# VectorE alone makes z and the late weights' low parts, in a new order of its queue

## The chip, the core and the metric

The kernel runs on one core of a Trainium2 chip. Its five queues (TensorE, VectorE, ScalarE, GpSimd, and SyncE for the transfers) each run their own instructions strictly in order and wait for one another through semaphores. The metric is the device time of one execution in microseconds; the text calls a time a median where it is one of several runs. In the profile PE is TensorE, PEld its weight loads, DVE VectorE, ACT ScalarE, POOL GpSimd, SP SyncE.

## The reference

Three layers, one after the other, on 4 sequences of 768 tokens and 384 channels:

```python
for t in range(S):                      # attention, 8 heads of 48
    y[:, :, t] = einsum(q[:, :, t], state)
    v_old = einsum(state, kt)
    state = state + bt * outer(kt, vt - v_old)
...
theta = x @ w_theta                     # mixing
zr, zi = x * np.cos(theta), x * np.sin(theta)
y = einsum('ts,bsd->btd', w_tok_r, zr) + einsum('ts,bsd->btd', w_tok_i, zi)
u = x + y
x = u + np.maximum(u @ w_ch, 0.0)
...
xn = (x - mu) / np.sqrt(var + 1e-06) * g_ln   # feed-forward
out = x + np.maximum(xn @ w_ch1, 0.0) @ w_ch2
```

The weights come as float64, the rest as float32.

## The kernel before

**Precision.** Each large product runs as three products of reduced-precision operands: a value is split into a high part (`hi`, `zh`, `xh`, a converting copy on ScalarE) and a low part (`lo`, `zl`, `xl`, the value minus its high part), and high x high, high x low and low x high are summed.

**Weights** (class `Weights`). The float64 words are turned to float32 on the chip, in units of two tiles of 128 x 384 (768 wide). A unit goes through three stages: its raw words are loaded and ScalarE takes their magnitude (`magnitude`, L759; in the attention VectorE does it itself, L755); VectorE clamps and merges the bits (`low`: two clamps, L765 and L766, two merges, L775 and L776); `parts` makes the high part (ScalarE, L789) and the low part (L794, VectorE or GpSimd by `split`). A call of `pump` moves each unit by one stage; a call of `step`, used in the attention, does half as much. `finish` does the last stage alone. Units of the mixing weights are called w0 to w5 by the tile of 128 source tokens that they serve, two units each. A unit of the feed-forward weights is only merged, multiplied by g on GpSimd (L784) and stored to memory (`stash`), to be loaded again as f0, f1, ... later.

**Attention.** Chunks c = 0 to 23 of 32 tokens. In each, `R` subtracts what the state already holds (VectorE's `Rs`, L427), for two halves of the heads, and the state's update on TensorE and ScalarE hangs on it. Between the halves a function `late(c, k)`, k = 0, 1, 2, puts preparations for the mixing into the queues.

**Mixing** (class `Mixer`, loop over 24 steps in `build`). The list MIX orders the steps: for each of four sequences b the source tiles s = 0, 1, 2, then for each the tiles 3, 4, 5. Step i multiplies z of (b, s) into six sums y, in two halves of 18 matmuls. Around that, the loop prepares ahead: `trans` transposes x of step i + 3, `theta` multiplies x of step i + 2 with w_theta, `angles` takes the fraction of a turn (`kk`, `nf`), `sines` and `cosines` evaluate it on ScalarE, and `turn` makes z of step i + 1 from it. After each third step the sums y go into u on VectorE and ScalarE (L929, L927). In the last steps the loop also starts the first column block of the feed-forward part (`pre`: parts, three products with the channel weights, mean, centring, square, reciprocal of the deviation).

**Feed-forward.** For eight column blocks and twelve weight tiles an up product, its positive part (`hh`, `hl`), and a down product.

The order of the loop's calls is the order of each queue. The numbers of calls in a step stand in two lists: PA[i] pumps before the first half of step i, PB[i] after its preparations.

Of the kernel before, what the change touches and what calls it, by code (L numbers as in the profile page):

```python
# [660 lines left out]
MAGIC = 12582912.0  # L661
# [11 lines left out]
class Weights:  # L673
# [32 lines left out]
    def pump(self):  # L706

        self.finish()
        for u in self.one:
            self.low(*u)  # L710
        self.one, self.two = [], self.one
        self.load()
        if self.loaded:
            u = self.loaded.pop(0)
            self.one.append(self.magnitude(*u))
        self.load()
        for dst, t in self.stores:
# [60 lines left out]
    def parts(self, u, raw, t, clamped):  # L778
        nc = self.nc
        self.ready.add(u[0])  # L780
        if len(u) == 5:
            dst, g = u[3:]
            w = t[:, 0].rearrange("p (k c) -> p k c", k=KB)
            nc.gpsimd.tensor_tensor(out=w, in0=w, in1=bc(g.unsqueeze(2), [128, KB, 128]), op=ALU.mult)  # L784
            self.stores.append((dst, t))
            return
        hi, lo, scale, split = u[3:]
        if scale is None:
            nc.scalar.copy(out=hi, in_=t)  # L789
            n = t.shape[1]  # L790
            split = n if split is None else split
            for e, r in ((nc.gpsimd, slice(0, split)), (nc.vector, slice(split, n))):
                if r.stop > r.start:
                    e.tensor_tensor(out=lo[:, r], in0=t[:, r], in1=hi[:, r].bitcast(F32), op=ALU.subtract)  # L794
        else:
            nc.scalar.activation(out=hi, in_=t, func=AF.Copy, scale=scale)
            nc.vector.scalar_tensor_tensor(out=lo, in0=t, scalar=scale, in1=hi.bitcast(F32), op0=ALU.mult, op1=ALU.subtract)


class Mixer:  # L800
# [19 lines left out]
    def load_w(self, s, wtok, pool, wts, w=None):  # L820
        w = self.W[s] = w or [pool.tile([128, 4, C], F32R, name=f"w{s}_{i}") for i in range(2)]
        for q in range(2):
            wts.add(("w", s, q), wtok[s, q], w[0][:, 2 * q:2 * q + 2], w[1][:, 2 * q:2 * q + 2], split=0 if s < 3 else None)
# [42 lines left out]
    def angles(self, i):  # L866
# [4 lines left out]
        nc.vector.tensor_scalar(out=kk, in0=ps, scalar1=MAGIC, scalar2=None, op0=ALU.add)  # L871
# [17 lines left out]
    def turn(self, i):  # L889
# [6 lines left out]
        nc.gpsimd.tensor_tensor(out=zf[:, 1], in0=zf[:, 1], in1=xs, op=ALU.mult)  # L896
        nc.vector.tensor_tensor(out=zf[:, 0], in0=zf[:, 0], in1=xs, op=ALU.mult)  # L897
        for q in range(2):
            nc.scalar.copy(out=zh[:, q], in_=zf[:, q])  # L899
            nc.gpsimd.tensor_tensor(out=zl[:, q], in0=zf[:, q], in1=zh[:, q].bitcast(F32), op=ALU.subtract)  # L900
        self.Z[i] = zh, zl

# [171 lines left out]
class Spare:  # L1074


    def __init__(self, st):
        self.st, self.n = st, 0

    def tile(self, shape, dt, name):  # L1080
        if name == "tot":
            return self.st.tile([128, 2, C], dt, name="t", bufs=3)[:, 0]
        if self.n % (4 * C) == 0:
            self.n = 0
            self.t = self.st.tile([128, 2 * C, 2], U32, name="raw", bufs=2).rearrange("p c t -> p (c t)")
        self.n += shape[1]
        return self.t[:, self.n - shape[1]:self.n].bitcast(dt)


def build(tc, a):  # L1090
# [8 lines left out]
    with tc.manual_schedule(), outer:  # L1099
# [14 lines left out]
        def late(c, k):  # L1114
# [16 lines left out]
            if (c > 19 or (c, k) == (19, 1)) and k < 2:  # L1131
# [51 lines left out]
        SLOTS = {"uh": 2, "ul": 3, "xh": 0, "xl": 1}  # L1183
# [17 lines left out]
        for i in range(n):  # L1201
# [32 lines left out]
            if i == 21:  # L1234
                two_f(0, *[slot(f"f0_{k}", 6 + k, [128, 4, C], F32R) for k in range(2)])
# [3 lines left out]
            for k in {15: (0,), 19: (4,), 20: (5,), 21: (6,), 22: (7,)}.get(i, ()):  # L1239
# [65 lines left out]
```

## Time and profile before

| what | value |
|---|---|
| median of three runs | 804.92 us (803.36 to 805.32) |
| the profiled execution | 804.83 us, of which the profile's span is 802.6 us |
| TensorE busy | 718.3 us, 89% of the span; granted clock 0.964 on average |
| VectorE busy | 527.6 us, 66% |
| ScalarE busy | 347.2 us, 43% |
| GpSimd busy | 302.7 us, 38% |

The span begins at the first instruction; all positions in the text are microseconds from there. Busy time of TensorE includes matmuls at half clock, so a busy TensorE may still lose time. The shares are averages over three layers with different limits, so the text goes by stretches of time.

### The profile page before, as it was taken

How to read it: one execution, taken by the hardware profiler on the slowest of the kernel's cores; microseconds unless marked ns; L12 is line 12 of the kernel's file. 1: busy time of each engine (PE TensorE's matmuls, PEld its weight loads, DVE VectorE, ACT ScalarE, POOL GpSimd, SP SyncE). 2: the span in 40 equal slices, each digit the busy share in tenths (PEclk: the TensorE clock that was granted, in tenths of full speed). 3: DMA queues.
4: the chain of work that ended last, by engine and by line, in shares of the span. 5: the costliest groups of instructions: out<-in, count | busy, mean ns of one | idle time of the engine just before them, and what ended most of it. 6: DMA issues, size and time to landing. Idle time of an engine off the chain costs nothing.

```text
span 802.6 us, 19216 instructions
## 1 busy us (share of the span) xinstructions
PE 718.3 (89%) x8059; PEld 658.3 (82%) x8062; DVE 527.6 (66%) x865; ACT 347.2 (43%) x783; POOL 302.7 (38%) x305
## 2 busy tenths in 40 slices
PE   4687877777777699999899899999999999999997
PEld 2465555554577689999799799999999999999997
DVE  5899899986778988889766645535343443444342
ACT  1276777687855455563434434222322222231310
POOL 4855655642223666565432533312111112112110
PEclk7599999999999999999999999999999999999999
DMA  9776657333453333433410220000000000000000
GB/s 269 222 206 187 208 165 223 90 83 120 152 177 119 119 105 93 127 130 101 155 40 21 98 84 16 31 1 31 1 30 0 31 1 20 11 1 30 1 30 29
DMA packets 29717, 71.41 MB, mean 89 GB/s; under 512 B 4928, under 2 KB 17472, under 8 KB 29632
## 3 DMA queue, kind: packets, MB, share of 16 engines
q1 hardware_dynamic: 29632, 70.19, 28.2%
q8 instruction: 63, 1.03, 0.5%
q14 instruction: 22, 0.18, 0.1%
HBM read 56.02 MB, written 9.44 MB: 82 GB/s over the span
## 4 chain that ended last, share of the span: by engine, by line
PE 53%; DVE 26%; ACT 8%; issue 6%; POOL 5%; DMA 1%; SPq 0%; ACTq 0%; DVEq 0%; POOLq 0%
PE ph L1034 19%; PE acc L1053 19%; PE pc L975 5%; DVE t L775 4%; PE y L920 4%; DVE t L776 3%; DVE prod L356 3%; ACT bdw L439 2%; DVE t L766 2%; DVE XT L365 2%; DVE t L765 2%; PE pth L862 1%; DVE zf L897 1%; POOL prodp L372 1%; POOL prodp L356 1%
## 5 line engine op out<-in xcount | busy, mean ns | idle before, releaser
L920 PE MATMUL y<-w,zh 128*128 128x384 f32 x576 | 157.6, 347 | 10.5 <-ACT w L789 7.1
L1053 PE MATMUL acc<-hh,f 128*128 128x384 f32 x576 | 147.0, 336 | 0.0
L1039 DVE SCALAR_TENSOR_TENSOR hl<-ph,hh 128x384 fp32r<-128x384 f32 x96 | 52.5, 554 | 114.8 <-ACT hh L1038 114.8
L1038 ACT ACTIVATE hh<-ph 128x384 fp32r<-128x384 f32 x96 | 46.8, 491 | 167.8 <-PE ph L1034 167.8
L920 PEld LDWEIGHTS y<-w,zh 128*128 128x128 f32 x576 | 108.0, 194 | 12.6 <-ACT w L789 7.8
L1034 PE MATMUL ph<-xh,f 128*128 128x384 f32 x576 | 116.4, 337 | 1.7 <-DVE u L929 1.7
L1053 PEld LDWEIGHTS acc<-hh,f 128*128 128x128 f32 x576 | 104.5, 188 | 0.0
L1034 PEld LDWEIGHTS ph<-xh,f 128*128 128x128 f32 x576 | 101.9, 188 | 2.0 <-issue 2.0
L920 PE MATMUL y<-w,zl 128*128 128x384 f32 x288 | 101.1, 351 | 1.0 <-POOL zl L900 0.6
L1053 PE MATMUL acc<-hl,f 128*128 128x384 f32 x288 | 96.9, 336 | 0.0
L900 POOL TENSOR_TENSOR zl<-zf,zh 128x384 fp32r<-128x384 f32 x48 | 64.5, 1365 | 50.7 <-ACT zh L899 50.7
L1034 PE MATMUL ph<-xl,f 128*128 128x384 f32 x288 | 65.7, 336 | 0.0
L439 ACT COPY bdw<-RW 32x192 f32<-32x192 f32 x192 | 59.6, 310 | 10.2 <-PE RW L435 7.6
L920 PEld LDWEIGHTS y<-w,zl 128*128 128x128 f32 x288 | 57.2, 199 | 2.6 <-POOL zl L900 2.6
L452 ACT COPY bds<-S 48x384 f32<-48x384 f32 x92 | 43.6, 474 | 29.7 <-PE S L447 28.3
L896 POOL TENSOR_TENSOR zf<-zf,x 128x384 f32<-128x384 f32 x24 | 27.4, 1141 | 73.3 <-ACT zf L879 73.2
L1053 PEld LDWEIGHTS acc<-hl,f 128*128 128x128 f32 x288 | 54.0, 188 | 0.0
L447 PE MATMUL S<-bdw,ktt 128*48 128x192 f32 x368 | 41.4, 348 | 13.8 <-ACT bdw L439 13.8
L1063 POOL TENSOR_TENSOR o<-u,o 128x384 f32<-128x384 f32 x21 | 20.8, 1021 | 85.0 <-DVE o L1062 85.0
L1034 PEld LDWEIGHTS ph<-xl,f 128*128 128x128 f32 x288 | 51.6, 188 | 0.0
L435 PEld LDWEIGHTS RW<-Rs,pt 32*32 32x32 f32 x1472 | 19.4, 107 | 30.8 <-DVE Rs L427 24.2
L447 PEld LDWEIGHTS S<-bdw,ktt 128*48 128x48 f32 x368 | 20.5, 126 | 27.8 <-ACT bdw L439 21.7
(159 smaller groups left out, 1342.4 us busy)
## 6 DMA issues: line engine op xcount, KB each, us to landing
kqt<-kq SPq DMA_DIRECT2D x20, 512.0 KB, 6.7
raw<-wtok SPq DMA_DIRECT2D x12, 768.0 KB, 4.3
raw<-wff SPq DMA_DIRECT2D x12, 768.0 KB, 5.0
bdk<-kq SPq DMA_DIRECT2D x40, 192.0 KB, 4.0
vt<-vin SPq DMA_DIRECT2D x24, 192.0 KB, 4.4
ktt<-ktok SPq DMA_DIRECT2D x24, 192.0 KB, 4.2
x<-ys SPq DMA_DIRECT2D x96, 48.0 KB, 2.8
flat<-t SPq DMA_DIRECT2D x12, 384.0 KB, 5.5
```

The lines of the kernel that those rows point to most:

```text
L356: eng.tensor_tensor(out=pr[:, j], in0=bc(lhs[:, j].unsqueeze(2), [128, i, c, kk]), in1=bc(rhs[:, j].unsqueeze(1), [128, i, c, kk]), op=ALU ...
L439: nc.scalar.copy(out=b[rr, :, r, :], in_=RW[h][rr, 1, :, :])
L447: nc.tensor.matmul(S_ps[h][64 * e:64 * e + D, g, :], KT[c][:, 2 * h + g, e, :], b[:, 2 * g + e, :, :], start=(c == 0 and g == 0), stop=Tru ...
L452: nc.scalar.copy(out=n[ee, :, e, :], in_=S_ps[h][ee, :, :].rearrange("p g (r d) -> p (g r) d", r=4))
L775: v.scalar_tensor_tensor(out=i, in0=raw[:, :, 1], scalar=0xC0000000, in1=i, op0=ALU.bitwise_and, op1=ALU.bitwise_or)
L900: nc.gpsimd.tensor_tensor(out=zl[:, q], in0=zf[:, q], in1=zh[:, q].bitcast(F32), op=ALU.subtract)
L920: nc.tensor.matmul(self.Y[q], l[:, ri, 128 * k:128 * k + 128], self.W[s][w][:, 2 * ri + h], start=(first and w == ri == 0 and l is zh), st ...
L975: nc.tensor.matmul(ps, self.wc[w][:, k, 128 * e:128 * e + 128], r[:, k], start=(n == 0), stop=(n == 8))
L1034: nc.tensor.matmul(ps, w[:, 0, 128 * k:128 * k + 128], r[:, k], start=(n == 0), stop=(n == 8))
L1038: nc.scalar.activation(out=hh, in_=ps, func=AF.Relu)
L1039: nc.vector.scalar_tensor_tensor(out=hl, in0=ps, scalar=0.0, in1=hh.bitcast(F32), op0=ALU.max, op1=ALU.subtract)
L1053: nc.tensor.matmul(self.ACC[j][e], w[:, 1, 128 * e:128 * e + 128], r, start=(f == 0 and n == 0), stop=(f == NF - 1 and n == 2))
```

## The change

`turn` multiplies both halves of z by x in one VectorE instruction and converts them in one ScalarE instruction; the subtraction for zl becomes `rest`, one VectorE instruction that stands behind the pumps of the step. `kk` moves from VectorE to ScalarE. The low parts of w0 and w1 go to GpSimd, those of w2 to w5 to VectorE. `pump` issues the high parts first, then clamps and merges, then the low parts, so that `parts` now returns the low part as a function. `finish` leaves the middle of the step. `step` is called at k = 2 too, the extra pumps of the first four steps (PB) fall away, and step 0 makes three before its first half (PA); the feed-forward tiles f0 and f1 are taken up in step 17 instead of 21, and mean, centring, square and reciprocal each come one step later.

```diff
     def pump(self):
-        self.finish()
+        lows = [self.parts(*u) for u in self.two]
         for u in self.one:
             self.low(*u)
         self.one, self.two = [], self.one
+        for f in lows:
+            f()
         self.load()
...
-                e.tensor_tensor(out=lo[:, r], in0=t[:, r], in1=hi[:, r].bitcast(F32), op=ALU.subtract)
+            def low():
+                for e, r in ((nc.gpsimd, slice(0, split)), (nc.vector, slice(split, n))):
+                    if r.stop > r.start:
+                        e.tensor_tensor(out=lo[:, r], in0=t[:, r], in1=hi[:, r].bitcast(F32), op=ALU.subtract)
...
-            wts.add(("w", s, q), wtok[s, q], w[0][:, 2 * q:2 * q + 2], w[1][:, 2 * q:2 * q + 2], split=0 if s < 3 else None)
+            wts.add(("w", s, q), wtok[s, q], w[0][:, 2 * q:2 * q + 2], w[1][:, 2 * q:2 * q + 2], split=0 if s > 1 else None)
...
-        nc.vector.tensor_scalar(out=kk, in0=ps, scalar1=MAGIC, scalar2=None, op0=ALU.add)
+        nc.scalar.activation(out=kk, in_=ps, func=AF.Identity, bias=self.magic)
...
-        nc.gpsimd.tensor_tensor(out=zf[:, 1], in0=zf[:, 1], in1=xs, op=ALU.mult)
-        nc.vector.tensor_tensor(out=zf[:, 0], in0=zf[:, 0], in1=xs, op=ALU.mult)
-        for q in range(2):
-            nc.scalar.copy(out=zh[:, q], in_=zf[:, q])
-            nc.gpsimd.tensor_tensor(out=zl[:, q], in0=zf[:, q], in1=zh[:, q].bitcast(F32), op=ALU.subtract)
+        nc.vector.tensor_tensor(out=zf, in0=zf, in1=bc(xs.unsqueeze(1), [128, 2, C]), op=ALU.mult)
+        nc.scalar.copy(out=zh, in_=zf)
         self.Z[i] = zh, zl
+        self.ZF2 = zf
+
+    def rest(self, i):
+        zh, zl = self.Z[i]
+        self.nc.vector.tensor_tensor(out=zl, in0=self.ZF2, in1=zh.bitcast(F32), op=ALU.subtract)
...
-            if (c > 19 or (c, k) == (19, 1)) and k < 2:
+            if c > 19 or (c, k) == (19, 1):
                 wts.step()
...
                 mx.turn(0)
+                mx.rest(0)
...
-        SLOTS = {"uh": 2, "ul": 3, "xh": 0, "xl": 1}
+        SLOTS = {"uh": 2, "ul": 3, "xh": 6, "xl": 7}
...
-        PA = [2] + [1] * 21 + [2] * 2
-        PB = [1] * 4 + [0] * 14 + [1] * 4 + [2] * 2
+        PA = [3] + [1] * 21 + [2] * 2
+        PB = [0] * 18 + [1] * 4 + [2] * 2
...
             for _ in range(PA[i]):
                 wts.pump()
+            if i + 1 < n:
+                mx.rest(i + 1)
             mx.mix(i, 0, yp)
-            wts.finish()
...
-            if i == 21:
-                two_f(0, *[slot(f"f0_{k}", 6 + k, [128, 4, C], F32R) for k in range(2)])
+            if i == 17:
+                two_f(0, *[slot(f"f0_{k}", k, [128, 4, C], F32R) for k in range(2)])
...
-            for k in {15: (0,), 19: (4,), 20: (5,), 21: (6,), 22: (7,)}.get(i, ()):
+            if i == 15:
+                wp.pool = ff.sp = Spare(mx.cst, ("w1_0", "w1_1"))
+            for k in {15: (0,), 20: (4,), 21: (5,), 22: (6,), 23: (7,)}.get(i, ()):
                 todo[k]()
```

What is left out moves the small tiles of `pre` into the tiles of w1, which are free by then, and keeps a feed-forward tile from being loaded before it is stored. Lines behind the edit shift by up to 16: the merges are L781 and L782 after, the clamps L771 and L772, Rs stays L427.

What the change moves is seen best on VectorE's queue, at three places. First the attention, from the second half of chunk 20 to the first half of chunk 22. Before:

```order
L427 TENSOR_TENSOR Rs_3763<-vt,RW_127 128x192
L797 SCALAR_TENSOR_TENSOR tw_3568<-t,tw_3567 128x768
L755 TENSOR_SCALAR t<-raw 128x384
L765 TENSOR_SCALAR t<-t 128x384
L766 TENSOR_SCALAR t<-t 128x384
L848 TENSOR_TENSOR xl<-pt,xh 128x384
L427 TENSOR_TENSOR Rs_3836<-vt,RW_126 128x192
L775 SCALAR_TENSOR_TENSOR t<-raw,t 128x384
L776 SCALAR_TENSOR_TENSOR t<-raw,t 128x384
L427 TENSOR_TENSOR Rs_3888<-vt,RW_127 128x192
```

And after:

```order
L807 SCALAR_TENSOR_TENSOR tw_3570<-t,tw_3569 128x768
L761 TENSOR_SCALAR t<-raw 128x384
L771 TENSOR_SCALAR t<-t 128x384
L772 TENSOR_SCALAR t<-t 128x384
L781 SCALAR_TENSOR_TENSOR t<-raw,t 128x384
L782 SCALAR_TENSOR_TENSOR t<-raw,t 128x384
L861 TENSOR_TENSOR xl<-pt,xh 128x384
L427 TENSOR_TENSOR Rs_3840<-vt,RW_126 128x192
L807 SCALAR_TENSOR_TENSOR tw_3570<-t,tw_3569 128x384
L761 TENSOR_SCALAR t<-raw 128x768
L771 TENSOR_SCALAR t<-t 128x768
L772 TENSOR_SCALAR t<-t 128x768
```

The next row there is `Rs_3898`. The merges of the second theta unit moved ahead of an Rs, and the clamps of the first unit of w0 (128x768) now stand ahead of the Rs of chunk 21's second half.

Second, step 0 of the mixing, from z of step 1 on. Before (w_1_3699 is the low part of w1, nf that of step 2):

```order
L897 TENSOR_TENSOR zf<-zf,x_70 128x384
L775 SCALAR_TENSOR_TENSOR t<-raw,t 128x768
L776 SCALAR_TENSOR_TENSOR t<-raw,t 128x768
L794 TENSOR_TENSOR w_1_3699<-t,w_0_3698 128x768
L765 TENSOR_SCALAR t<-t 128x768
L766 TENSOR_SCALAR t<-t 128x768
L775 SCALAR_TENSOR_TENSOR t<-raw,t 128x768
L776 SCALAR_TENSOR_TENSOR t<-raw,t 128x768
L794 TENSOR_TENSOR w_1_3699<-t,w_0_3698 128x768
```

After (w_1_4259 is the low part of w2):

```order
L909 TENSOR_TENSOR zf<-zf,x_70 128x768
L771 TENSOR_SCALAR t<-t 128x768
L772 TENSOR_SCALAR t<-t 128x768
L781 SCALAR_TENSOR_TENSOR t<-raw,t 128x768
L782 SCALAR_TENSOR_TENSOR t<-raw,t 128x768
L771 TENSOR_SCALAR t<-t 128x768
L772 TENSOR_SCALAR t<-t 128x768
L781 SCALAR_TENSOR_TENSOR t<-raw,t 128x768
L782 SCALAR_TENSOR_TENSOR t<-raw,t 128x768
L802 TENSOR_TENSOR w_1_4259<-t,w_0_4258 128x768
L916 TENSOR_TENSOR zl<-zf,zh 128x768
L885 SCALAR_TENSOR_TENSOR nf<-kk,pth 128x384
```

The units of w1 are gone from here, two units of w2 stand in their place, and zl of step 1, which GpSimd made before, stands behind them.

Third, a middle step with a unit of the feed-forward weights. Before:

```order
L897 TENSOR_TENSOR zf<-zf,x_71 128x384
L765 TENSOR_SCALAR t<-t 128x768
L766 TENSOR_SCALAR t<-t 128x768
L775 SCALAR_TENSOR_TENSOR t<-raw,t 128x768
L776 SCALAR_TENSOR_TENSOR t<-raw,t 128x768
L871 TENSOR_SCALAR kk<-pth 128x384
L872 SCALAR_TENSOR_TENSOR nf<-kk,pth 128x384
L852 TENSOR_TENSOR u_65<-u_65,pt 128x3x128
L848 TENSOR_TENSOR xl<-pt,xh 128x384
```

After:

```order
L909 TENSOR_TENSOR zf<-zf,x_71 128x768
L771 TENSOR_SCALAR t<-t 128x768
L772 TENSOR_SCALAR t<-t 128x768
L781 SCALAR_TENSOR_TENSOR t<-raw,t 128x768
L782 SCALAR_TENSOR_TENSOR t<-raw,t 128x768
L916 TENSOR_TENSOR zl<-zf,zh 128x768
L885 SCALAR_TENSOR_TENSOR nf<-kk,pth 128x384
L865 TENSOR_TENSOR u_65<-u_65,pt 128x3x128
L861 TENSOR_TENSOR xl<-pt,xh 128x384
```

z is whole, zl is new in the queue, kk has left it.

## Rows read from the trace of the kernel before

**Rows 1.** Busy time by stretch: us, then each engine's, granted clock, transfers.

```profile
core 0: us, PE busy (x) PEld busy (x) DVE busy (x) ACT busy (x) POOL busy (x), PEclk, DMA share, GB/s
196.00:225.00 29.00, 22.74 (x588) 15.86 (x588) 21.95 (x37) 24.78 (x63) 5.74 (x4) 1.00 0.38 118
225.00:303.00 78.00, 62.61 (x319) 59.61 (x320) 67.43 (x80) 40.11 (x73) 39.13 (x26) 0.91 0.40 139
303.00:382.70 79.70, 79.70 (x469) 79.00 (x468) 70.32 (x97) 41.09 (x81) 48.52 (x40) 1.00 0.37 108
436.00:458.40 22.40, 19.17 (x95) 17.22 (x93) 11.44 (x14) 10.24 (x16) 12.54 (x12) 0.92 0.25 89
458.40:802.60 344.20, 340.02 (x1945) 339.70 (x1945) 151.89 (x266) 88.83 (x174) 65.70 (x63) 1.00 0.06 20
```

**Rows 2.** The chain of waits, 385 to 460 us: start, us, what.

```profile
390.61 7.83 PE y L920 x36
...
400.00 1.56 PE pth L862 x9
401.56 0.33 PE pt L835 x3
401.89 6.26 PE y L920 x36
```

**Rows 3.** TensorE in order of time; in brackets idle time before, and releaser.

```profile
236.87 0.61 PE L920 MATMUL y<-w,zh 128*128 128x384 f32 x1 [3.10 <-ACT w L789]
...
390.06 0.55 PE L835 MATMUL pt<-ident,x 128*128 128x128 f32 x3 [3.02 <-DVE u L977]
...
458.36 0.93 PE L1034 MATMUL ph<-xh,f 128*128 128x384 f32 x4 [1.72 <-DVE u L929]
```

**Rows 4.** Busy time by stretch, just after the second of these waits.

```profile
390.60:394.00 3.40, 3.40 (x13) 3.40 (x12) 2.60 (x6) 2.04 (x4) 1.01 (x1) 0.50 0.90 227
```

**Rows 5.** VectorE in order of time, one steady step.

```profile
303.39 1.67 DVE L775 SCALAR_TENSOR_TENSOR t<-raw,t 128x768 uint32<-128x768 uint32 x1
...
307.25 0.55 DVE L872 SCALAR_TENSOR_TENSOR nf<-kk,pth 128x384 f32<-128x384 f32 x1
...
309.59 0.56 DVE L897 TENSOR_TENSOR zf<-zf,x 128x384 f32<-128x384 f32 x1 [1.32 <-POOL zf L896]
```

**Rows 6.** VectorE in order of time, early in the mixing.

```profile
232.82 0.55 DVE L765 TENSOR_SCALAR t<-t 128x768 f32<-128x768 f32 x1
...
235.00 0.96 DVE L776 SCALAR_TENSOR_TENSOR t<-raw,t 128x768 uint32<-128x768 uint32 x1
236.85 0.96 DVE L794 TENSOR_TENSOR w<-t,w 128x768 fp32r<-128x768 f32 x1 [0.90 <-ACT w L789]
237.73 0.55 DVE L765 TENSOR_SCALAR t<-t 128x768 f32<-128x768 f32 x1
```

**Rows 7.** GpSimd in order of time, in the steady step of rows 5.

```profile
302.92 3.02 POOL L900 TENSOR_TENSOR zl<-zf,zh 128x384 fp32r<-128x384 f32 x2 [1.25 <-ACT zh L899]
```

**Rows 8.** VectorE in order of time, end of the attention.

```profile
202.66 0.35 DVE L427 TENSOR_TENSOR Rs<-vt,RW 128x192 f32<-128x192 f32 x1 [0.72 <-PE RW L424]
...
216.96 0.35 DVE L427 TENSOR_TENSOR Rs<-vt,RW 128x192 f32<-128x192 f32 x1
```

**Rows 9.** SyncE's transfer queue in order of time.

```profile
200.28 0.53 SPq L699 DMA_DIRECT2D raw<-wtok  x1
...
227.47 1.92 SPq L699 DMA_DIRECT2D raw<-wtok  x2
```

**Rows 10.** Transfers by line: count, size, median us from issue to landing.

```profile
raw<-wtok SPq DMA_DIRECT2D x12, 768.0 KB, 4.3
```

**Rows 11.** ScalarE in order of time, end of the attention.

```profile
224.46 0.48 ACT L479 COPY ys<-py 128x384 f32<-128x384 f32 x1 [0.30 <-PE py L473]
```

**Rows 12.** VectorE in order of time, end of the mixing.

```profile
451.01 0.55 DVE L1016 TENSOR_SCALAR raw<-pst 128x384 f32<-128x384 f32 x1
...
456.42 1.33 DVE L1021 SCALAR_TENSOR_TENSOR rs<-t,rs 128x384 f32<-128x384 f32 x1 [1.13 <-POOL t L1020]
```

More of the change, by code (lines that the diff above doesn't have):

```diff
@@ L692, in load @@
         while self.todo and len(self.loaded) < (1 if self.more is None else 2):
+            if self.stores and not self.todo[0][2]:
+                return
             u = self.todo.pop(0)
@@ L718, in pump @@
             self.nc.sync.dma_start(out=dst, in_=t)
-        self.stores = []
+        if self.stores:
+            self.stores = []
+            self.load()
     def finish(self):
         for u in self.two:
-            self.parts(*u)
+            self.parts(*u)()
         self.two = []
@@ L785, in parts @@
             self.stores.append((dst, t))
-            return
+            return lambda: None
         hi, lo, scale, split = u[3:]
@@ L791, in parts, with low @@
             split = n if split is None else split
-            for e, r in ((nc.gpsimd, slice(0, split)), (nc.vector, slice(split, n))):
-                if r.stop > r.start:
-                    e.tensor_tensor(out=lo[:, r], in0=t[:, r], in1=hi[:, r].bitcast(F32), op=ALU.subtract)
+            def low():
+                for e, r in ((nc.gpsimd, slice(0, split)), (nc.vector, slice(split, n))):
+                    if r.stop > r.start:
+                        e.tensor_tensor(out=lo[:, r], in0=t[:, r], in1=hi[:, r].bitcast(F32), op=ALU.subtract)
         else:
             nc.scalar.activation(out=hi, in_=t, func=AF.Copy, scale=scale)
-            nc.vector.scalar_tensor_tensor(out=lo, in0=t, scalar=scale, in1=hi.bitcast(F32), op0=ALU.mult, op1=ALU.subtract)
+            def low():
+                nc.vector.scalar_tensor_tensor(out=lo, in0=t, scalar=scale, in1=hi.bitcast(F32), op0=ALU.mult, op1=ALU.subtract)
+        return low
 class Mixer:
@@ L814, in load_theta @@
         self.nc.gpsimd.memset(self.halfpi, HALF_PI)
+        self.magic = self.cst.tile([128, 1], F32, name="magic")
+        self.nc.gpsimd.memset(self.magic, MAGIC)
         self.tw = [self.cst.tile([128, KB, C], F32R, name=f"tw{i}") for i in range(2)]
@@ L1074, with __init__ @@
 class Spare:
-    def __init__(self, st):
-        self.st, self.n = st, 0
+    def __init__(self, pool, tags):
+        self.t = [pool.tile([128, 4, C], F32R if i == 0 else F32, name=t, tag=t) for i, t in enumerate(tags)]
+        self.n = [0, 0]
     def tile(self, shape, dt, name):
[L1081 to L1087, printed above, removed]
+        k = 0 if dt == F32R else 1
+        n = self.n[k]
+        self.n[k] += 1
+        return self.t[k][:, n]
 def build(tc, a):
@@ L1193, in build @@
         n = len(MIX)
-        PA = [2] + [1] * 21 + [2] * 2
-        PB = [1] * 4 + [0] * 14 + [1] * 4 + [2] * 2
+        PA = [3] + [1] * 21 + [2] * 2
+        PB = [0] * 18 + [1] * 4 + [2] * 2
         wp = Late()
-        wp.pool = ff.sp = Spare(wts.st)
         todo = first_pre = ff.pre(0, big, wp, psa)
```

## The prediction

> **What bounds the kernel now.** I read the busy time by stretch first [rows 1]. It splits the program in four. Until 225 us runs the attention. From 225 to 458 us runs the mixing, from 458 us to the end the feed-forward part, where TensorE is busy 340.0 of 344.2 us; the change moves only what stands at that part's very start, so I count the rest as it is. In the mixing TensorE is busy 79.7 of 79.7 us between 303 and 383 us, but only 62.6 of 78.0 us before, and 19.2 of 22.4 us at the end. Busy there is not full speed either: the granted clock is 0.91 in the early stretch. VectorE is busy 67.4 of the 78.0 us of the early stretch.
>
> How long would TensorE need if it never waited? The chain of waits shows its pieces [rows 2]: 36 mixing matmuls 6.26 us, a theta product of nine 1.56 us, three transposes 0.33 us, so 8.15 us for a full step, at the full clock of 2.4 GHz. 20 full steps of that (steps 1 to 20), step 21 without a transpose (7.8), steps 22 and 23 without theta (12.5), three products with the channel weights of the size of a theta (4.7) and two small sums (0.7) make 188.8 us after step 0, and with step 0 about 197. The stretch took 458.4 - 225.0 = 233.4 us. So 36 us are lost in it, and that is the most that the change can gain there.
>
> Where they go: TensorE waits for weight tiles, 3.10 us in one place, for a transpose buffer that VectorE frees late, 3.02 us, and 1.72 us at the start of the feed-forward part [rows 3]. After the 3.02 us the same 36 matmuls took 7.83 us [rows 2], with a granted clock of 0.50 [rows 4], the level of 1.2 GHz: the wait cost 1.57 us again. Behind all these waits stands VectorE. In a steady step it passes each of the two merges of the float64 words (L775, L776) in some 1.67 us [rows 5], while the same operation takes 0.96 us elsewhere [rows 6]. In the slow case GpSimd is in its subtraction for zl, 302.92 to 305.94 us [rows 7].
>
> **The change on VectorE, step by step.** GpSimd loses both halves of the z subtraction and the half multiplication. So the merges should go at 0.96 us, 1.4 us less for the pair. VectorE takes over z whole and zl whole; a 768-wide two-input operation passes in 0.88 us (236.85 to 237.73) [rows 6], so zl adds 0.88 and z 0.41 over its half. Its first theta instruction goes to ScalarE (minus 0.58). A weight unit of w3 to w5 brings its subtraction from GpSimd, 0.88. The sum of a step with a weight unit, by my count: z 0.88, clamps and merges 3.14 (232.82 to 235.96, [rows 6]), the unit's low part 0.88, zl 0.88, and from nf to the next z 2.34 (307.25 to 309.59, [rows 5]), in which ScalarE makes sine and cosine: 8.12 us. TensorE needs 8.15. A unit without low part gives 7.24. Where a batch ends, two or three additions into u come on top (0.47 each), so single steps go over 8.15, by about 0.9 in one of three; zl runs nearly 2 us ahead when the steady steps begin, because TensorE takes step 1 at a low clock (below), and I take 0.5 us of loss for all of them (bounds 0 and 3).
>
> The Trainium skill speaks to the 1.4 us: SBUF — State Buffer, section Who interferes with whom, says that a VectorE instruction with two SBUF inputs contends for the shared port pair with a GpSimd instruction that reads SBUF, and that the loser blocks. The rows above agree (0.96 and 1.67 us). By that rule, what GpSimd still has would cost VectorE the same kind of delay: four low parts of w0 and w1 in the attention.
>
> **The attention pays.** Four more preparation steps are called in it, at each third place of a chunk: one more unit merged (w10) and one more whole (w11). VectorE idles 29.0 - 21.95 = 7.05 us of 196 to 225 us [rows 1], and its added instructions are about 4 us after what moves away. But order counts. The state recurrence waits for one subtraction, Rs, and new work now stands ahead of it. First, the clamps of unit w00 now stand before the Rs that ran at 202.66 us [rows 8]. Their data are issued at 200.28 us [rows 9] and land 4.3 us later (median, [rows 10]), at 204.6; 1.7 us of clamping brings Rs to 206.3, 3.6 us late. About 0.6 of that comes back where theta used to be waited for. Second, before the Rs of 216.96 us [rows 8] now stand the merges of w10, z whole, ScalarE's conversion of z and zl: The half before is 3.1 late then (214.1); clamps 2.5 and merges 2.1 beside a GpSimd subtraction end at 218.7, the cosine, late too, at 219.5, and z, conversion and zl take 0.9 each: 222.3, 5.3 late. The last ys (224.46, [rows 11]) and with it the first mixing matmul come 5.5 us late, at 230.5. Bounds: 0, if the idle time hides all; 12, if the four GpSimd subtractions also stretch the operations beside them by the ratio of 1.67 to 0.96.
>
> **A new wait in step 1.** Three pumps stand in step 0 between z of step 1 and zl of step 1, and they work on w2, whose load is issued only after the last x transfer, 2.5 us behind ys (224.94 to 227.47) [rows 9, 11]. Landing 230.4 + 2.5 + 4.3 = 237.2; then ScalarE's magnitude 0.9, two units of clamps and merges 2 x 3.14, one low part 0.88, zl 0.88: 246.2 us. Step 0 keeps TensorE busy until 230.5 + 8.3 = 238.8. So TensorE waits 7.4 us there, and what stands behind the wait is the whole mixing; the clock cost of 1.57 follows, as after the 3.02 us. In exchange the two waits for w1 and w2 (3.10 and another) are gone, since w1 is complete before the mixing and w2 before step 2.
>
> **The late steps.** In step 16 the transposes still wait for VectorE to free a buffer. TensorE wants it 6.3 us into the step (half the mixing, channel product, theta); VectorE starts z at 1.7, after the three ul, and z, merges, zl and the freeing addition bring it to 7.2: 0.9 us of wait instead of 3.02. In step 18 it starts at 0.7, but two clamps of an extra pump (1.2) stand between: 7.4, so 1.1. Together 2.0 (bounds 0 and 4.6). At the end the tiles f0 and f1 are ready steps earlier, and the square root and reciprocal come after step 23 instead of before it. Two things are late then. The zl of step 23 stands behind three centring rounds of three operations of about 0.55 us, like nf [rows 5]: with z, its conversion and zl it is there 7.7 us after the start of step 22, which lasts 6.3: 1.4 us of wait. And the first hl of the feed-forward part stands behind the chain of the reciprocal, 6.7 us from 451.01 to 457.75 [rows 12]: with one addition before and hl itself 7.8 us after the last mixing matmul, while TensorE has three up products and two small pieces, 5.4 us, to cover it: 2.4 us of wait. 3.8 together, for 3.2 us idle and some 1.7 lost to the clock of 0.92 [rows 1] before (bounds 1 and 7).
>
> **Sum.** 246.2 + 188.8 + 1.6 + 0.5 + 2.0 + 3.8 = 442.9 for the first up product, which ran at 458.4 [rows 3]: 15.5 us less. The profiled execution took 804.83 us, 0.09 below the median of 804.92, so I forecast 789 us. About 0.3% (2.4 us) is what this kernel's timing can tell from no change.
>
> **Rivals.**
> 1. *VectorE becomes the bound of every mixing step, and the kernel is slower.* The merges stay at 1.67 us, because their slowness has another cause than GpSimd (the transfers or ScalarE are busy in these places too). Then a step is 9.5 us, 22 steps lose 22 x 1.38 less 2 of lead = 28 us against the forecast: 817. It decides from a step of about 8.9 us on (15.5 / 22, and the lead, over 8.15). For it: the margin of 0.03 us a step is nothing. Against: wherever GpSimd is idle, the rows show 0.96. Chance 0.08.
> 2. *The attention pays its upper bound and the late steps keep today's waits.* 6.5 + 4 more: 799, in a band from 794 to 802. For it: the recurrence has many small waits that a late Rs can shift. Chance 0.20.
> 3. *The added steps hide in the attention, and the tail waits do not appear.* 5.5 and 2.5 less: 781, in a band from 776 to 784. For it: 7 us of idle time. Against: Rs stands in the same queue. Chance 0.19.
> 4. *Nothing comes of it*: the wait of step 1 grows to about 23 us, since w2 lands late (three loads at once). 804, within 0.3%. Chance 0.06.
> The forecast, 784 to 794, has 0.47.
>
> **Numbers.** The range from 780 to 801 leaves out the slow rival, half of the fourth and the ends of the two bands, together 0.2. Faster by over 0.3%: 0.47 + 0.20 + 0.19 = 0.86; same 0.06; slower 0.08.
>
> **What would show it.** The L775 and L776 of before should stand at 0.96 us in nearly all steps; if they stay at 1.67, rival 1. TensorE's first mixing matmul should start near 230 us, wait once for about 7 us after step 0 and then hold 8.15 us a step until step 16. The last Rs should be 5 us late; if it is on time, rival 3. The first up product should start near 443 us. I am wrong if VectorE's zl is what TensorE waits for in more than two steps, or if the attention is longer by over 8 us.

## The result, and the profile after

The changed kernel takes 793.35 us (median of 4 runs, 792.07 to 795.23) where the kernel before, beside it, took 804.25 (4 runs, 803.36 to 805.32): the ratio is 0.9866, with a 95% interval from 0.9837 to 0.9895. A second set of runs of the same two kernels (e11 below) gave 0.9865, from 0.9842 to 0.9889. So the change takes off about 11 us. The forecast was 789, in a range from 780 to 801: right in kind, and 4.4 us too hopeful.

The profiled execution of the changed kernel has a span of 790.3 us. Busy time by stretch, with the columns and the stretches of [rows 1]:

```profile
195.00:229.30 34.30, 24.14 (x587) 16.65 (x587) 27.76 (x41) 27.39 (x66) 6.52 (x4) 0.95 0.37 123
229.30:303.00 73.70, 66.14 (x378) 65.53 (x379) 58.83 (x82) 45.46 (x79) 2.20 (x2) 0.95 0.33 115
303.00:382.70 79.70, 78.57 (x461) 77.97 (x460) 68.00 (x102) 45.84 (x80) 13.31 (x9) 1.00 0.40 125
419.50:441.90 22.40, 20.57 (x117) 19.99 (x116) 14.33 (x25) 9.98 (x15) 5.11 (x5) 1.00 0.00 1
441.90:790.30 348.40, 341.81 (x1946) 341.17 (x1944) 153.90 (x266) 89.34 (x175) 66.38 (x63) 0.99 0.07 23
...
242.10:249.00 6.90, 3.56 (x11) 3.56 (x12) 5.65 (x9) 3.43 (x8) 0.00 (x0) 0.51 0.61 211
...
450.20:453.90 3.70, 3.70 (x14) 3.70 (x13) 0.70 (x2) 0.83 (x1) 0.82 (x1) 0.54 0.84 306
```

GpSimd's 39.1 us of the early stretch have become 2.2. The last line of the first block is the news: the feed-forward part is 348.4 us long, not 344.2, and it contains a piece at half clock (450.2 to 453.9).

TensorE in order of time, the waits that answer to [rows 3]:

```profile
229.32 0.44 PE L935 MATMUL y<-w,zh 128*128 128x384 f32 x1 [0.55 <-ACT ys L479]
...
245.44 0.69 PE L935 MATMUL y<-w,zl 128*128 128x384 f32 x1 [7.54 <-DVE zl L916]
...
377.19 0.55 PE L848 MATMUL pt<-ident,x 128*128 128x128 f32 x3 [1.13 <-DVE u L992]
...
398.46 0.55 PE L848 MATMUL pt<-ident,x 128*128 128x128 f32 x3 [1.49 <-DVE u L992]
...
434.25 0.44 PE L935 MATMUL y<-w,zh 128*128 128x384 f32 x1 [1.28 <-ACT zh L910]
435.24 0.45 PE L935 MATMUL y<-w,zl 128*128 128x384 f32 x1 [0.55 <-DVE zl L916]
...
441.87 1.20 PE L1049 MATMUL ph<-xh,f 128*128 128x384 f32 x6
...
449.47 0.44 PE L1068 MATMUL acc<-hl,f 128*128 128x384 f32 x1 [2.41 <-DVE hl L1054]
...
453.92 0.51 PE L1068 MATMUL acc<-hh,f 128*128 128x384 f32 x2
```

One long wait opens the mixing, four short ones stand at its end, and 2.41 us come after the first up product. Between the first and the second of these waits TensorE runs through. VectorE in order of time, z of one of those steps and then the next from its z to its zl, as in [rows 5, 6]:

```profile
247.50 0.96 DVE L909 TENSOR_TENSOR zf<-zf,x 128x768 f32<-128x768 f32 x1 [1.18 <-ACT zf L900]
...
255.37 0.96 DVE L909 TENSOR_TENSOR zf<-zf,x 128x768 f32<-128x768 f32 x1 [1.18 <-ACT zf L900]
256.24 0.55 DVE L771 TENSOR_SCALAR t<-t 128x768 f32<-128x768 f32 x1
256.83 0.56 DVE L772 TENSOR_SCALAR t<-t 128x768 uint32<-128x768 uint32 x1
257.43 0.96 DVE L781 SCALAR_TENSOR_TENSOR t<-raw,t 128x768 uint32<-128x768 uint32 x1
258.42 0.96 DVE L782 SCALAR_TENSOR_TENSOR t<-raw,t 128x768 uint32<-128x768 uint32 x1
259.30 0.95 DVE L802 TENSOR_TENSOR w<-t,w 128x768 fp32r<-128x768 f32 x1
260.17 0.95 DVE L916 TENSOR_TENSOR zl<-zf,zh 128x768 fp32r<-128x768 f32 x1
```

The merges stand at 0.96 us. From one z to the next are 7.87 us (247.50 to 255.37).

**Where the time went.** The attention's first 185 us are the same code in both kernels and yet differ between executions: the last Rs ahead of every changed instruction starts between 183.88 and 187.21 us in the profiles of this document. So I measure stages from that Rs, which started at 186.15 us before and at 184.97 after:

| stage, us | before | forecast | after |
|---|---|---|---|
| that Rs to the first mixing matmul | 38.85 | 44.35 | 44.36 |
| first mixing matmul to first up product | 233.37 | 212.4 | 212.55 |
| first up product to the end | 344.25 | 344.25 | 348.43 |
| sum | 616.47 | 601.0 | 605.34 |

Each entry is the difference of two starts in the trace; the forecast's are 38.85 + 5.5, 442.9 - 230.5, and unchanged. The change won 20.8 us in the mixing, paid 5.5 in the attention and gave 4.2 back behind the mixing: 11.1 in all.

### The profile page after: what moved, and what is told of

It is laid out like the page before. It is cut to its first block, busy times and chain, and to the rows that moved or that the text cites. A ratio compares the mean times of both kernels' runs of the same rounds, so it can differ in the third digit from the quotient of the medians.

```text
span 790.3 us, 19137 instructions
## 1 busy us (share of the span) xinstructions
PE 709.3 (90%) x8059; PEld 654.2 (83%) x8062; DVE 518.8 (66%) x868; ACT 356.7 (45%) x782; POOL 212.2 (27%) x232
## 4 chain that ended last, share of the span: by engine, by line
PE 68%; DVE 16%; ACT 7%; issue 3%; DMA 3%; POOL 2%; SPq 1%; ACTq 0%; DVEq 0%; POOLq 0%
PE acc L1068 19%; PE ph L1049 19%; PE y L935 14%; PE pc L990 4%; PE pth L875 3%; ACT bdw L439 3%; DVE prod L356 3%; PE S L447 2%; DVE XT L365 1%; PE py L473 1%; DMA raw<-wtok 1%; PE RW L435 1%; DVE t L781 1%; DVE u L944 1%; DVE Ti L365 1%
## 5 line engine op out<-in xcount | busy, mean ns | idle before, releaser
L935 PE MATMUL y<-w,zh 128*128 128x384 f32 x576 | 154.1, 341 | 1.8 <-ACT zh L910 1.3
L935 PEld LDWEIGHTS y<-w,zh 128*128 128x128 f32 x576 | 105.4, 189 | 2.4 <-ACT zh L910 1.6
L935 PE MATMUL y<-w,zl 128*128 128x384 f32 x288 | 98.3, 341 | 8.1 <-DVE zl L916 8.1
L935 PEld LDWEIGHTS y<-w,zl 128*128 128x128 f32 x288 | 55.0, 191 | 8.7 <-DVE zl L916 8.7
L790 POOL TENSOR_TENSOR t<-t,g 128x384 f32<-128x384 f32 x12 | 16.9, 1411 | 137.9 <-DVE t L782 134.8
L1078 POOL TENSOR_TENSOR o<-u,o 128x384 f32<-128x384 f32 x21 | 20.8, 1017 | 85.0 <-DVE o L1077 85.0
L435 PE MATMUL RW<-Rs,pt 32*32 32x48 f32 x1472 | 25.8, 208 | 16.3 <-DVE Rs L427 16.2
```

The costliest lines, as they stand in the source:

```text
L435: nc.tensor.matmul(RW[h][rr, 1, j, :], PT[c // 4][rr, m0 + j, :], Rs[rr, j, :], start=True, stop=True)
L935: nc.tensor.matmul(self.Y[q], l[:, ri, 128 * k:128 * k + 128], self.W[s][w][:, 2 * ri + h], start=(first and w == ri == 0 and l is zh), st ...
```

## Experiments

Theory A: GpSimd's work on SBUF stretched VectorE's merges, and freeing them is the gain. Its rival, theory B: the merges were slow for another reason, and the new order or the earlier weights are the gain. A second question is where the missing 4.4 us are. All ratios are to runs of the kernel before on the same chip. The stages of each profiled execution, cut as above:

| run | attention | mixing | rest | ratio, 95% interval |
|---|---|---|---|---|
| e11, the changed kernel again | 45.39 | 212.31 | 347.54 | 0.9865 (0.9842 to 0.9889) |
| e1 | 45.31 | 225.09 | 347.20 | 1.0019 (0.9995 to 1.0042) |
| e2 | 46.17 | 212.66 | 347.34 | 0.9858 (0.9827 to 0.9890) |
| e3 | 44.46 | 210.73 | 348.42 | 0.9831 (0.9792 to 0.9869) |
| e4 | 40.03 | 215.28 | 347.63 | 0.9823 (0.9789 to 0.9857) |
| e5 | 45.96 | 212.44 | 344.88 | 0.9838 (0.9804 to 0.9871) |
| e6 | 40.47 | 215.19 | 347.47 | 0.9822 (0.9792 to 0.9852) |
| e7 | 45.44 | 212.81 | 347.19 | 0.9894 (0.9867 to 0.9921) |
| e8 | 41.53 | 214.54 | 346.08 | 0.9819 (0.9788 to 0.9850) |
| e9 | 40.32 | 212.28 | 344.89 | 0.9778 (0.9757 to 0.9799) |
| e10 | 44.70 | 210.69 | 344.99 | 0.9804 (0.9784 to 0.9824) |
| e12 | 40.09 | 211.37 | 345.01 | 0.9747 (0.9717 to 0.9776) |

The intervals are some 3 to 6 us wide, so differences of 2 us between these runs are read from the stages, not from the ratios.

### e1 and e2: GpSimd beside the merges again

```diff
                 mx.turn(i + 1)
+                if 3 <= i <= 10:
+                    xs = x[MIX[i + 1][1]][:, MIX[i + 1][0]]
+                    for _ in range(4):
+                        nc.gpsimd.tensor_tensor(out=xs, in0=xs, in1=xs, op=ALU.subtract)
```

e2 has `nc.gpsimd.memset(xs, 0.0)` in the last line.

> The changed kernel with four GpSimd subtractions of 384 columns added in each of the mixing steps 3 to 10; they start when z is made and write only x that nobody reads again, so no queue but GpSimd's own gets anything new and nothing waits for them. Theory A (the merges were slow because GpSimd works on SBUF beside them): clamps, merges, low part and zl in these eight steps go from 0.56 and 0.96 us towards 1.2 and 1.67, a VectorE step from 7.9 to 9.3 to 10.8 us, above TensorE's 8.15; eight steps lose 1 to 2.5 us each, so 800 us (797 to 806) against 793. Theory B (the merges were slow from the transfers or ScalarE, and the reordering is what helped): merges stay at 0.96 and the time at 793 within 2.

> The same places, but GpSimd only fills the same columns four times with zero, so it writes SBUF and reads nothing. If every GpSimd instruction on SBUF slows VectorE: merges beside a fill at some 1.67 us, and a loss in proportion to the time that the fills take (3 to 10 us if they take 0.5 to 1 us each). If it is GpSimd's reading that VectorE loses to: merges at 0.96 us and 793 within 2. Theory B of the run with subtractions: also 793.

VectorE in order of time in a step of e1, then GpSimd in that step, then TensorE's waits:

```profile
305.61 0.96 DVE L909 TENSOR_TENSOR zf<-zf,x 128x768 f32<-128x768 f32 x1 [1.18 <-ACT zf L900]
...
307.07 1.06 DVE L772 TENSOR_SCALAR t<-t 128x768 uint32<-128x768 uint32 x1
308.17 1.47 DVE L781 SCALAR_TENSOR_TENSOR t<-raw,t 128x768 uint32<-128x768 uint32 x1
309.67 1.47 DVE L782 SCALAR_TENSOR_TENSOR t<-raw,t 128x768 uint32<-128x768 uint32 x1
311.06 1.57 DVE L802 TENSOR_TENSOR w<-t,w 128x768 fp32r<-128x768 f32 x1
```

```profile
306.71 5.11 POOL L1222 TENSOR_TENSOR x<-x 128x384 f32<-128x384 f32 x4 [4.90 <-DVE zf L909]
```

```profile
282.59 0.44 PE L935 MATMUL y<-w,zl 128*128 128x384 f32 x1 [1.57 <-DVE zl L916]
292.60 0.44 PE L935 MATMUL y<-w,zl 128*128 128x384 f32 x1 [1.56 <-DVE zl L916]
303.55 0.44 PE L935 MATMUL y<-w,zl 128*128 128x384 f32 x1 [2.51 <-DVE zl L916]
```

The merges went from 0.96 to 1.47 us, and from z to z are 10.0 us (295.60 to 305.61), above TensorE's 8.15; TensorE now waits for zl in step after step. The mixing is 12.5 us longer. Eight of the 24 steps with GpSimd at work take the whole gain away. Over these steps 32 of VectorE's 768-wide operations stand 17.1 us in all above 0.56 us (clamps) and 0.96 us (the others). In the kernel before it was 16.0 us for 19 operations between 225 and 303 us, as in these two clamps, and in the changed kernel 0.6 us for one:

```profile
275.49 2.21 DVE L765 TENSOR_SCALAR t<-t 128x768 f32<-128x768 f32 x1
277.73 2.04 DVE L766 TENSOR_SCALAR t<-t 128x768 uint32<-128x768 uint32 x1
```

The delays alone cost nothing: between 303 and 383 us the kernel before had 12.5 us of them too, and TensorE was busy 79.7 of 79.7 us there [rows 1]. They cost time only where VectorE has none to spare: in the early steps before, and in e1. In e2 the same places hold fills:

```profile
301.51 0.74 DVE L772 TENSOR_SCALAR t<-t 128x768 uint32<-128x768 uint32 x1
302.29 0.96 DVE L781 SCALAR_TENSOR_TENSOR t<-raw,t 128x768 uint32<-128x768 uint32 x1
```

```profile
301.13 2.44 POOL L1222 MEMSET x<- 128x384 f32 x4 [5.61 <-DVE zf L909]
```

The merge that runs beside the last two fills (302.29) keeps its 0.96 us, the mixing its length. Only the second clamp is longer, 0.74 for 0.56. Theory A holds, and more narrowly: it is GpSimd's reading. The Trainium skill says this too (SBUF — State Buffer, Who interferes with whom): an instruction with two SBUF inputs contends with a GpSimd instruction that reads SBUF, not with one that only writes. For the merges both runs agree (1.47 and 0.96 us); the clamp at 0.74 us beside a fill has one input and is not explained by it.

### e3: zl of step 1 ahead of the preparation calls

```diff
+            if i == 0:
+                mx.rest(1)
             for _ in range(PA[i]):
                 wts.pump()
-            if i + 1 < n:
+            if 0 < i and i + 1 < n:
                 mx.rest(i + 1)
```

> The changed kernel with zl of step 1 put ahead of the three preparation calls of step 0, nothing else. Theory P (the 7.5 us wait of step 1 is a matter of position: zl stands behind merges that nobody needs yet): the wait goes, and the clock's 1.8 us with it, 784. Theory Q (VectorE is out of time there, 8.1 us of work a step and w2 landing late): step 1 starts without a wait, but z of step 2 comes only after the merges, at about 247.5 us, its conversion at 248.4 and, behind the next merges, its zl at 252.3, where TensorE wants them at 246.1; so a wait of about 6 us appears one step later, and the time is 792 (790 to 794).

The 7.54 us are gone, and TensorE waits in the same step for something else:

```profile
247.13 2.26 PE L875 MATMUL pth<-tw,xh 128*128 128x384 f32 x6 [4.51 <-DVE nf L885]
```

The theta of step 3 needs the PSUM buffer that nf of step 2 reads, and nf stands behind the merges of w2 as zl did. The mixing is 1.8 us shorter. Theory Q had the sum right and the place wrong: work of VectorE was late, not one instruction.

### e4 and e7: what the attention pays for

```diff
-            if c > 19 or (c, k) == (19, 1):
+            if (c > 19 or (c, k) == (19, 1)) and k < 2:
-        PA = [3] + [1] * 21 + [2] * 2
+        PA = [3, 2] + [1] * 20 + [2] * 2
```

> The changed kernel without the preparation steps at the third place of a chunk, so that w1 is merged in the mixing: three calls in step 0 and two in step 1, from there on the same state as in the changed kernel. My account of the price: the attention gets its 5.3 us back (first mixing matmul 5 us earlier), zl of step 1 then stands behind w1 and the first half of w2 and TensorE waits about 4 us, 1.3 us more in step 2, and 1.7 us by the clock: 7 us lost there where the changed kernel loses 9.3; the time is 786 (783 to 790). Rival (the weights made ready in the attention are what makes the change fast): VectorE falls behind by the two units of 3.1 us each and their landing, the waits of steps 1 and 2 grow to 12 us or more, and the time is 794 to 800.

The attention is 4.3 us shorter than in the changed kernel, the mixing 2.7 longer: 2.4 us less in the profiles where I had expected 7. (The five runs without the added steps have 40.0 to 41.5 us of attention, the eight profiles with them 44.4 to 46.2.) The zl of step 1 came 7.63 us late instead of 4. VectorE and GpSimd in e4 show why:

```profile
231.47 2.51 DVE L781 SCALAR_TENSOR_TENSOR t<-raw,t 128x768 uint32<-128x768 uint32 x1
...
236.07 2.48 DVE L781 SCALAR_TENSOR_TENSOR t<-raw,t 128x768 uint32<-128x768 uint32 x1
```

```profile
231.06 2.11 POOL L802 TENSOR_TENSOR w<-t,w 128x768 fp32r<-128x768 f32 x1 [8.13 <-ACT w L795]
235.92 1.82 POOL L802 TENSOR_TENSOR w<-t,w 128x768 fp32r<-128x768 f32 x1 [2.75 <-ACT w L795]
```

Two merges stood for 1.5 us each behind GpSimd's low parts of w1, which I had forgotten. The rival (the early weights are the gain) is refuted: without the added steps the kernel is no slower (0.9823 for 0.9866). In e7 GpSimd makes no low part of w0 and w1 at all:

```diff
-... split=0 if s > 1 else None)
+... split=0)
```

> The changed kernel with the low parts of w0 and w1, too, on VectorE, so that GpSimd does nothing for the weights in the attention. If the stretching of VectorE's work beside these GpSimd subtractions (2.18, 2.54 and 1.93 us seen where 0.56, 0.96 and 0.55 stand elsewhere) is what the attention pays with: 4.8 us come off and four low parts of 0.95 us, some of them in idle time, go on, so the first mixing matmul comes 1 to 3 us earlier and the time falls by as much. If the price is data that land late and the order ahead of the two Rs: no change within 1 us.

The attention stays at 45.4 us. So taking GpSimd out of the attention gains nothing. But e7 does not tell how much of the price is stretching (L772 at 2.18 us, L781 at 2.54 in the changed kernel): two of the low parts that VectorE takes over stand ahead of the second of the two Rs, and wait there 0.97 and 1.53 us for ScalarE. That late data and order make most of the price, as the forecast had it, is read from VectorE's queue. VectorE in the changed kernel, where [rows 8] had Rs at 202.66 and 216.96:

```profile
202.94 0.56 DVE L761 TENSOR_SCALAR t<-raw 128x768 uint32<-128x768 uint32 x1 [1.31 <-DMA raw<-wtok]
...
204.60 0.35 DVE L427 TENSOR_TENSOR Rs<-vt,RW 128x192 f32<-128x192 f32 x1
...
215.11 2.54 DVE L781 SCALAR_TENSOR_TENSOR t<-raw,t 128x768 uint32<-128x768 uint32 x1
217.68 0.96 DVE L782 SCALAR_TENSOR_TENSOR t<-raw,t 128x768 uint32<-128x768 uint32 x1
218.58 0.96 DVE L909 TENSOR_TENSOR zf<-zf,x 128x768 f32<-128x768 f32 x1
220.44 0.96 DVE L916 TENSOR_TENSOR zl<-zf,zh 128x768 fp32r<-128x768 f32 x1 [0.90 <-ACT zh L910]
221.31 0.34 DVE L427 TENSOR_TENSOR Rs<-vt,RW 128x192 f32<-128x192 f32 x1
```

Counted from the common Rs, the first is 3.1 us later than before and the second 5.5. Ahead of the first stand 1.31 us of wait for data and three operations of the unit at their normal 0.56, so nothing is stretched there; of the 2.4 us that the second adds, up to 1.6 can be the stretched merge at 215.11.

### e5: the chain of the reciprocal moved away

```diff
+        def sums():
+            hold["ps"] = bcast("v")
         def rstd():
-            ps = bcast("v")
+            ps = hold.pop("ps", None) or bcast("v")
...
-            for k in {15: (0,), 20: (4,), 21: (5,), 22: (6,), 23: (7,)}.get(i, ()):
+            for k in {15: (0,), 20: (4,), 21: (5,), 22: (6,), 23: (8,)}.get(i, ()):
...
-            if j and f == 3:
+            if f == (3 if j else 4):
                 last[7]()
```

> The changed kernel with the square root and reciprocal of the first tile moved behind five up products of the feed-forward part; only its two small sums stay behind the mixing. Theory (the 4 us missing from the forecast are the wait for the first hl, 2.41 us, and the half clock after it, some 1.7 us, which the forecast's sum did not have): hl comes at about 444.6 us, ahead of the 447.1 at which TensorE wants it, the wait and the drop of the clock go, 4 us less than the changed kernel, 0.9815 of the kernel before. Rival (VectorE is late there anyway, with six additions into u and two low parts ahead of hl, or the chain stalls the later hl just as long): under 1 us less.

The first hl came at 444.57 us (444.6 expected), the wait of 2.41 and the half clock are gone, and one wait of 0.46 us for a weight's low part is left (0.31 in e11). The part after the first up product is 344.88 us, against 348.43 in the profile of the changed kernel and 347.54 in e11, where the clock did not fall. The theory holds in the profiles; the ratio's interval holds both theory and rival.

### e6 and e8: the start in another order, and both together

```diff
-        PA = [3] + [1] * 21 + [2] * 2
-        PB = [0] * 18 + [1] * 4 + [2] * 2
+        PA = [2] + [1] * 11 + [2] + [1] * 9 + [2] * 2
+        PB = [1] + [0] * 17 + [1] * 4 + [2] * 2
...
+            if i == 0:
+                mx.rest(1)
             for _ in range(PA[i]):
                 wts.pump()
-            if i + 1 < n:
+            if 0 < i and i + 1 < n:
                 mx.rest(i + 1)
+            if i < 2:
+                wts.finish()
```

In addition w1's low parts go to VectorE, step 0 makes no clamps ahead of theta, and the added steps of the attention are left out as in e4. e8 adds the edit of e5, and `22: (5, 6)` for `21: (5,), 22: (6,)`.

> The changed kernel without the preparation steps at the third place of a chunk, and with the first two mixing steps written in the order in which TensorE needs things: zl of step 1 ahead of all merges, w1 finished in step 0 with its low parts on VectorE, nf and xl ahead of w2's merges, and the merges of w3 to w5 one step later (one call more in step 12). Theory (the waits of steps 1 and 2, 9.3 us with two preparation steps, are the order of VectorE's queue and two merges stretched to 2.5 us beside GpSimd's low parts of w1): waits of about 1 us in step 1 and 2 us in step 2, no drop of the clock, so 7 us less than with two preparation steps alone, 0.974 of the kernel before. Rival (VectorE has more work than time until step 3, in whatever order): the wait moves into theta of step 1 or z of step 2, and it is 0.981 to 0.983.

> The reordered start and the late square root together, and the three centring rounds moved from step 21 to step 22, behind z and zl of step 23. If the three losses are independent: 7 us from the start, 4 from the chain of the reciprocal and 1.8 from the waits for zh and zl of step 23, against the kernel with two preparation steps: 0.967 of the kernel before. If the centring rounds now make the first up product wait instead, 1 to 2 us of that is given back.

Both fell short: e6 gave 0.9822 where 0.974 was expected, e8 0.9819 for 0.967. The first two waits of e6 are 1.43 and 2.39 us, nearly as expected, instead of 7.63 and 1.66. And yet the mixing is 215.2 us: the extra call in step 12 cost four waits for zl and nf (0.27, 0.31, 0.95 and 0.51 us), and the transposes of step 16 wait 2.87 us; e9, without that call, has none of these. VectorE has that little to spare. In e8 the later centring made the small sum late that stands ahead of the first up product, a wait of 1.93 us where it had saved 1.83.

### e9, e10 and e12: versions without these losses

e9 leaves out the extra call (`PA = [2] + [1] * 21 + [2] * 2`) and splits the centring: its small sum stays behind step 21, its rounds on VectorE come in step 22 behind zl. e10 is the changed kernel with the tail of e9 alone. e12 is e9 with zl ahead of the low parts in steps 1 and 21.

> The reordered start and the late reciprocal of e6 and e8, but without the extra call in step 12 (every later unit, the channel weights too, stays one step later), and with the small sum that the centring needs left behind step 21 on TensorE while VectorE's three centring rounds stand behind zl of step 23. Theory (e6 and e8 lost again what they had won, some 3.8 us by the extra merges in step 12 and 1.9 us by a sum that came too late): from the first mixing matmul to the first up product 209.5 us (e8: 214.5), from there to the end 344.9 (e8: 346.1), so 6 us less than e8, 0.974 of the kernel before. Rival (VectorE has no time to spare until step 20, so one step less of lead must be paid somewhere, at the channel weights in step 16 or at f1): the same as e8, 0.982.

> The changed kernel with the tail alone mended: the late reciprocal, and VectorE's centring rounds behind z and zl of step 23. Theory: the start as in the changed kernel (first mixing matmul to first up product 212.5 less the waits for zh and zl of 1.28 and 0.55: 210.7), 344.9 from there; so 5.4 us less than the changed kernel, 0.980 of the kernel before. Rival: the centring, now later, makes the first up product wait 1 to 2 us: 0.982.

> The changed kernel itself once more beside the same runs of the kernel before, for a narrower interval: 0.9866 again (0.984 to 0.989). The forecast's 15.9 us would be 0.980.

e10 came out as expected in every stage: 210.69 and 344.99 us, 0.9804. e9 missed its mixing by 2.8 us, by a wait that was not there before: in step 22, zl stood behind a low part of f1 and took 1.75 us beside a GpSimd low part, and TensorE ran at half clock behind the wait. The channel weights in step 16 cost 0.73 and 0.76 us more. TensorE in e9, step 22:

```profile
424.16 0.69 PE L935 MATMUL y<-w,zl 128*128 128x384 f32 x1 [2.55 <-DVE zl L916]
```

> The version of e9 with one thing more: in steps 1 and 21, zl stands ahead of the low parts of the weight unit of its step, which TensorE needs later or not at all yet. If these waits are the order of VectorE's queue: the 2.39 us in step 2 become 1.4 and the half clock behind them (1.3 us) goes; the 2.55 us in step 22, where the zl took 1.75 us beside a GpSimd low part, become 1 or less, and the half clock behind them (1.7) goes too; from the first mixing matmul to the first up product 206.7 us (e9: 212.3), 0.971 of the kernel before. If zh, not zl, is late there: 1 to 2 us less at most, 0.976.

In e12 that wait is 0.55 us, and the one in step 2 is 1.51 without a drop of the clock behind it. But the mixing is only 0.9 us shorter than in e9 (4.7 short of the 206.7): the wait for w1 in step 1 was 1.83 us instead of 0.84, and the clock fell in step 22 all the same (last section). At 785.45 us, 0.9747, e12 is the fastest of all; against e9 the intervals overlap.

## Why the prediction was right, and where it was off

**The bound and its cause.** Right. e1 and e2 show that GpSimd's reading is enough to make VectorE the bound again, with everything else of the change in place: the merges go to 1.47 us beside reads and stay at 0.96 beside fills. Rival 1 (they stay at 1.67) fell with the first profile. What the new order adds by itself was not tried apart.

**The attention's price.** 5.5 forecast, 5.51 measured, through the two Rs named: 3.1 later for 3.6, 5.5 for 5.3. The exact match is luck: in the eight profiles that kept these steps the price is 5.5 to 7.3 us, 6.4 in the mean. That it comes from late data and order is read from the queue; e7 does not separate it from the stretching. Rival 3, that the steps hide there, is refuted; of rival 2, the attention's price stayed far from its bound of 12, and the late waits shrank. e4 shows what the forecast didn't ask: the added steps cost more there than they win in the mixing.

**Step 1.** 7.54 us of wait for 7.4, and the half clock behind it as forecast: 17 matmuls in 4.85 us instead of some 3.2. From the first mixing matmul to the end of that wait are 16.1 us, for 15.7. Rival 4 did not come.

**The steady steps.** From 251.94 to 366.30 us lie 14 steps, 8.17 us each: 0.3 us lost for 0.5.

**The late steps.** 1.13 + 1.49 = 2.6 us, for 2.0. Within the bounds.

**The tail is the term that failed.** The waits themselves were named and nearly sized: 1.28 + 0.55 for zh and zl of step 23 (1.4 forecast), 2.41 for hl (2.4). But the sum put the 2.4 ahead of the first up product and then let the feed-forward part stand at its 344.2 us, with "the change moves only what stands at that part's very start". The wait lies behind three up products, inside that part. And the step took the lost clock off the tail of before without asking what a wait of 2.4 us does to the clock of after: in the profiled execution the 16 matmuls behind it took 4.45 us (449.47 to 453.92), and in e11, where the clock stayed full, 2.89 (450.54 to 453.43, last section). The tail in all is 2.4 us too long ahead of the first up product (steps 22 and 23 take 14.96 us, from 426.56 to 441.52, for 2 x 6.26) and 4.2 behind it, 6.6 for 3.8. That the first up product still came within 1 us of the forecast's time is an accident: the mixing ran over by about as much as had been counted there wrongly.

**The sum of the misses.** From start to start each wait costs 0.2 to 0.3 us more than the idle time in brackets. Theta and transposes take 1.81 us in a steady step and 3.17 and 3.53 in steps 16 and 18, so the late steps lose 3.1 us, for 2.0. That is 2.8 us in the tail, 1.1 in the late steps and 0.4 in steps 0 and 1, less 0.2 in the steady steps: 4.1 of the 4.4 us. The rest I could not place. From the first mixing matmul on, e5 is 3.7 us shorter than the profile of the changed kernel and 2.5 shorter than e11, e10 5.3 and 4.2: so much of the tail can be had.

## What to carry to other kernels

When two engines overlap, ask which of GpSimd's instructions read SBUF while VectorE runs two-input operations; taking them away can be worth more than the work they did, where VectorE is late, and giving such work back in a third of the steps (four of 1 to 1.4 us in each) cost all of it here. Where an in-order engine has only 0.3 us a step to spare, moving one instruction forward moves the wait to the next thing behind the same work (e3, e6); what pays is to leave out of the early steps what nobody needs yet. And a sum of waits must say on which side of each milestone a wait falls, and what the clock does behind it.

## What the runs showed of the hardware that was not expected

**One long GpSimd instruction stops one VectorE instruction.** Beside a 768-wide GpSimd subtraction of 1.8 to 2.1 us a single merge or clamp takes about 1.4 to 1.6 us more, and a merge behind it is at its normal 0.96. Beside 384-wide ones, each merge takes 0.5 (e1) to 0.7 us (the kernel before) more, and in e1 GpSimd's own go from 1.01 to 1.43 us.

**The same wait does not always cost the clock.** In the eight profiles that kept the reciprocal's chain in its place TensorE waited 2.4 to 2.5 us for the same hl. In the execution of the changed kernel shown above and in e3 the granted clock then fell to half; in the other six (e11, e1, e2, e4, e6, e7) it stayed full. And in e12 it fell after 1.07 and 0.55 us of wait in step 22, while 1.28 and 0.55 in step 23 of the changed kernel left it at 1.00. Stretches of e12, of the changed kernel and of e11, with the columns of [rows 1], and TensorE in e11:

```profile
422.00:424.00 2.00, 1.45 (x6) 1.19 (x7) 2.00 (x2) 1.10 (x2) 1.04 (x1) 0.86 0.00 0
424.00:426.00 2.00, 2.00 (x8) 2.00 (x7) 0.62 (x2) 1.31 (x3) 0.00 (x0) 0.50 0.04 8
```

```profile
434.00:436.00 2.00, 1.20 (x5) 0.95 (x6) 0.96 (x1) 1.26 (x2) 0.66 (x1) 1.00 0.00 0
436.00:438.00 2.00, 2.00 (x14) 2.00 (x13) 0.00 (x0) 0.52 (x2) 1.37 (x2) 1.00 0.00 0
```

```profile
452.00:454.00 2.00, 2.00 (x14) 2.00 (x13) 0.00 (x0) 0.38 (x1) 0.00 (x0) 1.00 0.98 352
```

```profile
450.54 0.45 PE L1068 MATMUL acc<-hl,f 128*128 128x384 f32 x1 [2.52 <-DVE hl L1054]
...
453.43 0.51 PE L1068 MATMUL acc<-hh,f 128*128 128x384 f32 x2
...
455.98 0.79 PE L1049 MATMUL ph<-xh,f 128*128 128x384 f32 x3 [0.31 <-POOL f L802]
```

Why one falls and the other doesn't, these runs don't tell. What is shown is the price: some 1.4 to 1.8 us each time in the matmuls behind the wait. At the end less of it is left here. The part after the first up product is 348.4 us in the two executions with the fall and 347.2 to 347.6 in the six without: TensorE, being earlier, waits soon after for a weight's low part (455.98 in e11).
